# A joint network's forward and backward pass: rows of the second chunk by TensorE transposes, fe transposes planned later, grad x by two taps per matmul, last gradients reordered

## The chip, the core and the metric

The kernel runs on one core of a Trainium2 chip. A core has five engines that work side by side, each through its own queue in order: TensorE (matmuls into PSUM; PE in the profile, its weight loads PEld), VectorE (DVE), ScalarE (ACT), GpSimd (POOL) and SyncE (SP), which here only issues transfers. Transfers are carried out by 16 DMA engines that all queues share. The metric is the device time of one execution in microseconds (us).

## The reference

The kernel computes the forward pass below and the gradients of all seven inputs for a given `grad_out` (eight outputs in bfloat16). x is [2, 16000, 256], g is [2, 8, 256], and w1 and w2 have three taps of 256x256.

```python
h = gelu(conv3(x, w1))[:, ::2, :]          # tanh form of gelu; [2, 8000, 256]
f = gelu(conv3(h, w2))[:, ::2, :]          # [2, 4000, 256]
fe = einsum("btd,de->bte", f, w_f)
ge = einsum("bud,de->bue", g, w_g)
j = tanh(fe[:, :, None, :] + ge[:, None, :, :])   # [2, 4000, 8, 256]
out = einsum("btud,dv->btuv", j, w_o)
# and vjp of this: grads of x, w1, w2, g, w_f, w_g, w_o
```

## The kernel before

**Tiling.** The 2 x 4000 steps t of the output are cut into 17 chunks: the first of 256 steps, fifteen of 512, the last of 64. A chunk has A blocks (2, 4, 1) of at most 128 steps. Each chunk goes through three stages. Stage a (`stage_a`) computes the two convolutions with their gelu (`conv_gelu`): HTo and HTe (odd and even rows of h), FT (f), then FE (fe). All of these have features on partitions and steps along the free axis. Stage j (`stage_j`) forms j for the eight u, writes the output, and multiplies `grad_out` back to the gradient NGFE of fe. Stage de (`stage_de`) goes back through both convolutions: GF, GHe and GHo are the gradients before the gelus, `wgrad` adds the weight gradients up, and grad x is written row by row. The main loop over k puts stage j of chunk k beside stage a of chunk k+1 and stage de of chunk k-1.

**The order is planned.** Every operation is a call of `op` with an engine (or two that it may run on), a cost in ns, what it reads and writes, and a due time (`at`, else `F.now`). `Flow.issue` then simulates the engines with these costs, and at each step takes the operation that can start earliest, among equals the one due first; the order found is the program's order on each engine. An operation can start when what it depends on is done (`ready`). So a change of a cost, or of one operation, can move others in the queues far behind it. Transfers are `op`s too, on SP, ACT or POOL (`dma`).

**Two forms of j.** The output and the elementwise gradients need j with features on partitions: JT, by ACT's tanh of FE with ge as bias (L643). The gradient of w_o needs j with steps on partitions as well, the rows JR: two halves of the blocks for each of four pairs of u, so eight JR of 128x1024 in a full chunk. For chunks in `TRANS` they come from JT by TensorE transposes and one copy from PSUM (L662 and `evac`, L345 on ACT or L350 on DVE). For the other chunks TensorE transposes FE once (`rows`, L489), a copy makes FER, and then DVE adds ge's rows (L667) and ACT takes tanh again (L672). Before, `TRANS` is (0,). JR and grad_out's rows GO then go into the sum GWO in PSUM.

**What else the change touches.** `conv_gelu` takes Square (L510) and Gelu (L512) of each of two PSUM tiles, both due at `F.now`, Square first. Grad x (four rows per block) is made in pairs of rows: the first pair is GHo·tap0 + GHe·tap2 and GHo·tap1, the second pair is GHe'·tap0 + GHo·tap2 and GHe'·tap1 (GHe' is the block one further); each product has two halves of the contraction, so a pair takes six matmuls of 256 columns, into the two halves of one PSUM tile. In the chunk with the batch border, GHz, a copy of GHe with a zeroed column, stands for GHe' in tap 0 of block 0. Then the three taps of grad w1 follow. In the last chunk `acc_add` makes each weight gradient's final value by one DVE operation (L763) into a staging tile, and SP stores it.

Of the kernel before, what the change touches and what calls it, by code (L numbers as in the profile page):

```python
# [31 lines left out]
class Op:  # L32
    __slots__ = ("eng", "cost", "fn", "deps", "soft", "succ", "left", "prio", "new", "bufs", "done", "work", "n",
                 "ready", "kind", "span")


class Flow:
# [29 lines left out]

    def op(self, eng, cost, fn, r=(), w=(), new=(), at=None, work=0.0, after=(), kind=None, behind=(), sub=None):
        o = Op()
# [3 lines left out]
        o.prio = ((self.now if at is None else at) + self.shift.get((self.stage, sub), 0.0), o.n)  # L73
        o.succ, o.done, o.ready, o.kind, o.span = [], None, 0.0, kind, None
        deps, bufs = set(after), []
# [31 lines left out]
    def issue(self):  # L107
# [12 lines left out]
        def put(o):  # L120
            o.ready = max((d.span[0] if d in o.soft else d.done for d in o.deps), default=0.0)
            for e in o.eng:
                avail[e].append(o)
# [97 lines left out]
def kernel(  # L221
# [20 lines left out]
    B, T, D = x.shape  # L242
# [20 lines left out]
    SHIFT = {}  # L263
    TRANS = (0,)

# [214 lines left out]

    def rows(k, cls, name, SRC, lo, n, r, at=None, pe=0):
        R = buf(cls, [P, n if cls != "hro" else NB + 1, D], BF16, name)
        if pe:
            tr = psum(BF16)

            def trs(e):
                for a in range(n):
                    for kt in range(KT):
                        nc.tensor.transpose(out=tr[:pe, a * D + kt * P:a * D + (kt + 1) * P], in_=SRC[:, lo + a, kt, :pe],  # L489
                                            identity=ident[:])  # L490
            op("PE", c_pe([P] * (n * KT)), trs, r=(r or [SRC]) + [ident], w=[tr], new=[tr], at=at)
            evac(lambda: R[:pe, 0:n].rearrange("p a d -> p (a d)"), lambda: tr[:pe, 0:n * D], n * D, r=[tr], w=[R], new=[R], f=0.58)
            return R
        dma("SP", lambda: R[:, 0:n].rearrange("p a (k d) -> p (a k) d", d=P),
            lambda: SRC[:, lo:lo + n].rearrange("p a k c -> p (a k c)"), r=[SRC] if r is None else r, w=[R],
            bytes_=n * 65536, new=[R], transpose=True, at=at)
        return R

    def conv_gelu(c, taps, rd, h_buf, h_lo, g_buf, g_lo, news):
# [3 lines left out]
        for mt in range(KT):  # L503
            ps = psum()

            def mms(e, mt=mt, ps=ps):
# [3 lines left out]
            op("ACT", c_act(W, True), lambda e, mt=mt, ps=ps: nc.scalar.activation(  # L510
                out=sq[:, 0:A, mt, :Pw], in_=fl(ps[:, :W], A), func=ACT.Square, scale=GELU_SQRT_K), r=[ps], w=[(sq, mt)])
            op("ACT", c_act(W, True), lambda e, mt=mt, ps=ps: nc.scalar.activation(  # L512
# [24 lines left out]
    def stage_a(k, t0, dt):  # L537
# [53 lines left out]
        if k not in TRANS:  # L591
            S["FER"] = rows(k, "fer", "FER", FE, 0, A, [(FE, 0), (FE, 1)], pe=Pw)
        F.now = t0 + 0.5 * dt
# [163 lines left out]
    def acc_add(ACC, key, acc_ap, ps, k, out):  # L757
        if k == NG - 1:
            t_ = buf({id(ACCF): "jr", id(ACC2): "jt", id(ACC1): "go"}[id(ACC)], [P, 2 * D], BF16, "stage")

            def flat():
# [3 lines left out]
                op0=ALU.mult, op1=ALU.subtract), r=[(ACC, key), ps], w=[t_], new=[t_])  # L765
            dma("SP", lambda: out.rearrange("(dt p) n -> p dt n", p=P),
                lambda: flat().rearrange("p (k d) -> p k d", d=D), r=[t_], w=[], bytes_=131072)
# [7 lines left out]
    def stage_de(k, t0, dt):  # L775
# [112 lines left out]
        if c.px is not None:  # L888
# [5 lines left out]
                r=[GHz], w=[GHzR], bytes_=65536, transpose=True)  # L894
        rows4 = [[(GHo, 0, 0), (GHe, 0, 2)], [(GHo, 0, 1)], [(GHe, 1, 0), (GHo, 0, 2)], [(GHe, 1, 1)]]
        GX = None
        for bl, m in c.sblk:
            if bl % 2 == 0:
                GX = buf("gx", [P, 2, 4, D], BF16, "GX_SB")
            for cp in range(2):  # L900
                ps = psum()
                jobs = []
                for cj in range(2):
                    l = [(SRC, off, i, kt) for SRC, off, i in rows4[2 * cp + cj] for kt in range(KT)]
                    jobs += [(cj, n == 0, n == len(l) - 1) + a for n, a in enumerate(l)]

                def mms(e, jobs=jobs, ps=ps, bl=bl, m=m):
                    for cj, s_, e_, SRC, off, i, kt in jobs:
                        src = SRC[:, off + bl, kt, :m]
                        if GHz is not None and bl == 0 and off == 1 and i == 0:  # L910
                            src = GHz[:, kt, :m]
                        mm(ps[:m, cj * D:(cj + 1) * D], src, W1T[:, kt, i * D:(i + 1) * D], s_, e_)
                op("PE", c_pe([D] * len(jobs)), mms, r=[GHo, GHe, W1T] + ([GHz] if GHz is not None else []), w=[ps],
                   new=[ps] + ([GX] if cp == 0 and bl % 2 == 0 else []))
# [3 lines left out]
            if bl % 2 == 1 or bl == A - 1:  # L918
# [14 lines left out]
                if c.ext and h == 0:  # L933
                    put(Pw, Pw + 1, 0, 3)
        for i in range(KK):
            def xl(da):
                return lambda a, m, d2: X[:m, 4 * a + da, d2 * P:(d2 + 1) * P]

            def he(a, m, i=i):
                return GHzR[:m, :] if GHzR is not None and i == 0 and a == 0 else GHeR[:m, a, :]  # L940
            wgrad(ACC1, i, lambda i=i: ACC1[:, i],
                  [(xl(i), rr(GHoR), c.sblk, [X, GHoR]),
                   (xl(i + 2), he, c.sblk, [X, GHeR] + ([GHzR] if GHzR is not None else []))], out_2[i])
            tick()

# [182 lines left out]
```

## Time and profile before

| what | us |
|---|---|
| median of three runs (lowest, highest) | 798.06 (797.32, 798.76) |
| the profiled execution, its own time | 797.41 |
| its span in the profile | 795.6 |
| busy: TensorE, VectorE, ScalarE, GpSimd | 774.8, 725.2, 720.7, 67.5 |
| mean granted TensorE clock | 0.996 of full speed |
| read from and written to memory | 51.42 and 50.34 MB |

The span begins with the first instruction and ends with the last; the execution's own time has about 1.8 us more around it. A busy TensorE is not TensorE at its peak: the ends of matmuls are modelled and overlap (one of 512 columns stands with 0.379 us while the next starts 0.216 us after it). So work on TensorE is counted here by the pitch from start to start, taken from rows with many matmuls. A row of the profile names line, engine, operation, output and inputs, then shapes, times and, in brackets, idle time before it and what ended it.

### The profile page before, as it was taken

What the parts mean: (1) busy time and instruction counts of PE and PEld (TensorE: products, weight loads), DVE (VectorE), ACT (ScalarE), POOL (GpSimd) and SP (SyncE); (2) the same over time, 40 slices, a digit from 0 to 9 for tenths busy, and PEclk for the clock granted to TensorE, in tenths of its full rate; (3) what the DMA queues carried; (4) which work ended last, traced back from release to release, by engine and by line L of the source; (5) the groups of instructions that cost most, each with busy time, mean ns of one, the idle gap of its engine ahead of it and who ended that gap; (6) DMA issues with size and microseconds to landing.
All of it is one profiled execution on the core that took longest, in us unless ns stands there. A gap on an engine that the chain in (4) does not pass through costs nothing.

```text
span 795.6 us, 16104 instructions
## 1 busy us (share of the span) xinstructions
PE 774.8 (97%) x5916; PEld 559.2 (70%) x5916; DVE 725.2 (91%) x1535; ACT 720.7 (91%) x1164; POOL 67.5 (8%) x227
## 2 busy tenths in 40 slices
PE   7989899999999999999999999999999999999996
PEld 6657578676776767768576685767868677687875
DVE  5899999998989989899998998989989999999964
ACT  6999999999898998989989899898999989899742
POOL 2020100101000010210100001010010100102010
PEclk9999999999999999999999999999999999999999
DMA  9999999999999999999999999999999999899994
GB/s 195 213 193 206 249 233 230 259 220 221 218 248 234 231 220 205 238 248 214 230 250 239 202 225 219 242 251 229 216 235 254 235 212 212 211 261 202 261 205 123
DMA packets 381811, 178.85 MB, mean 225 GB/s; under 512 B 307586, under 2 KB 375460, under 8 KB 379812
## 3 DMA queue, kind: packets, MB, share of 16 engines
q1 hardware_dynamic: 380788, 177.16, 99.7%
q8 instruction: 46, 0.75, 0.4%
q10 hardware_dynamic: 784, 0.39, 0.2%
q14 instruction: 33, 0.27, 0.1%
q0 software_dynamic: 160, 0.27, 0.1%
HBM read 51.42 MB, written 50.34 MB: 128 GB/s over the span
## 4 chain that ended last, share of the span: by engine, by line
PE 55%; ACT 24%; DVE 14%; issue 4%; DMA 3%; SPq 0%; DVEq 0%; ACTq 0%
PE ps L336 45%; PE GWO L336 8%; ACT JT L643 5%; ACT JR L672 4%; ACT JSQ L702 4%; ACT OUT_SB L345 3%; DVE g_s L515 3%; DVE NGZ L715 2%; ACT GX_SB L347 2%; ACT g_sq L510 1%; DVE ZS L732 1%; DMA GO<-in_grad_out_dram 1%; PE psb L489 1%; DMA out_dram<-OUT_SB 1%; DVE ACC L771 1%
## 5 line engine op out<-in xcount | busy, mean ns | idle before, releaser
L643 ACT ACTIVATE JT<-FE,GE 128x512 bf16<-128x512 bf16 (+4 forms) x288 | 190.7, 723 | 0.3 <-PE ps L336 0.3
L715 DVE SCALAR_TENSOR_TENSOR NGZ<-JSQ,ps 128x512 f32<-128x512 bf16 (+3 forms) x252 | 152.3, 613 | 1.6 <-PE ps L336 1.5
L336 PE MATMUL ps<-WO,JT 128*128 128x256 bf16 (+1 forms) x1008 | 150.0, 274 | 0.7 <-ACT JT L643 0.6
L336 PE MATMUL ps<-GOT,WOT 128*128 128x512 bf16 (+2 forms) x544 | 149.3, 363 | 0.4 <-DMA GOT<-GO 0.4
L672 ACT ACTIVATE JR<-JR 128x1024 bf16<-128x1024 bf16 (+1 forms) x124 | 136.2, 1101 | 12.8 <-DVE JR L667 12.8
L345 ACT CAST OUT_SB<-ps 128x512 bf16<-128x512 f32 (+1 forms) x215 | 132.7, 629 | 12.7 <-PE ps L336 12.5
L336 PEld LDWEIGHTS <-JT 128*128 128x128 bf16 (+1 forms) x1008 | 98.8, 98 | 57.9 <-issue 1.3
L702 ACT ACTIVATE JSQ<-JT 128x1024 bf16<-128x1024 bf16 (+2 forms) x123 | 128.7, 1046 | 10.0 <-DVE NGZ L715 7.7
L336 PE MATMUL GWO<-GO,JR 128*128 128x256 bf16 (+1 forms) x1008 | 131.4, 274 | 4.5 <-ACT JR L672 4.3
L732 DVE TENSOR_TENSOR ZS<-ZS,NGZ 128x1024 f32<-128x1024 f32 (+2 forms) x102 | 115.8, 1135 | 0.5
L336 PEld LDWEIGHTS <-JR 128*128 128x128 bf16 (+1 forms) x1008 | 98.0, 98 | 24.1 <-ACT JR L672 6.3
L336 PEld LDWEIGHTS <-W 128*128 128x128 bf16 x612 | 57.9, 98 | 59.7 <-issue 2.8
L515 DVE SCALAR_TENSOR_TENSOR g_s<-g_sq,ps 128x512 bf16<-128x512 bf16 (+2 forms) x102 | 65.1, 641 | 34.0 <-ACT HTo L512 32.7
L667 DVE TENSOR_TENSOR JR<-FER,GEB 128x1024 bf16<-128x1024 bf16 (+1 forms) x124 | 84.1, 684 | 3.1 <-PE GWO L336 2.3
L336 PE MATMUL ps<-XC,W 128*128 128x512 bf16 (+2 forms) x408 | 84.5, 362 | 1.7 <-DMA XC<-in_x_dram 1.7
L336 PEld LDWEIGHTS <-X 128*128 128x128 bf16 (+1 forms) x756 | 73.9, 98 | 9.0 <-DMA HRo<-HTo 0.2
L771 DVE TENSOR_TENSOR ACC<-ACC,ps 128x512 f32<-128x512 f32 x90 | 60.8, 684 | 20.1 <-PE ps L336 19.3
L336 PE MATMUL ps<-W1T,GHo 128*128 128x256 bf16 (+1 forms) x378 | 72.1, 273 | 0.0
L336 PE MATMUL ps<-W1T,GHe 128*128 128x256 bf16 (+1 forms) x376 | 71.8, 273 | 0.0
L510 ACT ACTIVATE g_sq<-ps 128x512 bf16<-128x512 f32 (+2 forms) x102 | 62.2, 610 | 8.6 <-PE ps L336 6.0
L336 PEld LDWEIGHTS <-WOT 128*128 128x128 bf16 x544 | 51.8, 98 | 22.9 <-DMA GOT<-GO 0.7
L347 ACT ACTIVATE GX_SB<-ps 128x512 bf16<-128x512 f32 (+1 forms) x98 | 59.2, 640 | 5.4 <-PE ps L336 4.9
(139 smaller groups left out, 1123.4 us busy)
## 6 DMA issues: line engine op xcount, KB each, us to landing
GO<-in_grad_out_dram SPq DMA_DIRECT2D x60, 512.0 KB, 5.6
out_dram<-OUT_SB SPq DMA_DIRECT2D x60, 512.0 KB, 6.1
X<-in_x_dram SPq DMA_DIRECT2D x15, 1088.0 KB, 7.4
out_dram<-GX_SB SPq DMA_DIRECT2D x30, 512.0 KB, 4.5
GO<-in_grad_out_dram SPq DMA_DIRECT2D x5, 256.0 KB, 5.3
GOT<-GO SPq DMA_TRANSPOSE x65, 4.7
out_dram<-OUT_SB SPq DMA_DIRECT2D x4, 256.0 KB, 3.5
XC<-in_x_dram SPq DMA_TRANSPOSE x62, 4.4
```

Of the source, the lines that this page charges most:

```text
L336: nc.tensor.matmul(ps_ap, lhsT=lhsT, rhs=rhs, start=start, stop=stop)
L345: nc.scalar.copy(out=dst(), in_=src())
L347: nc.scalar.activation(out=dst(), in_=src(), func=ACT.Copy, scale=scale)
L510: op("ACT", c_act(W, True), lambda e, mt=mt, ps=ps: nc.scalar.activation(out=sq[:, 0:A, mt, :Pw], in_=fl(ps[:, :W], A), func=ACT.Square, s ...
L515: op("DVE", c_dve(W), lambda e, mt=mt, ps=ps: nc.vector.scalar_tensor_tensor(out=s[:, 0:A, mt, :Pw], in0=sq[:, 0:A, mt, :Pw], scalar=1.0, ...
L643: nc.scalar.activation(out=fl(JT[:, j, mt, :W], A)[:, :, lo:hi], in_=FE[:, 0:A, mt, lo:hi], func=ACT.Tanh, bias=GE[:, b, mt, 2 * up + j:2 ...
L667: op("DVE", c_dve(n * 2 * D, 0.5), lambda e, lo=lo, n=n, m=m, JR=JR: nc.vector.tensor_tensor(out=JR[:m, 0:n], in0=S["FER"][:m, lo:lo + n]. ...
L672: op("ACT", c_act(n * 2 * D), lambda e, n=n, m=m, JR=JR: nc.scalar.activation(out=JR[:m, 0:n], in_=JR[:m, 0:n], func=ACT.Tanh), r=[JR], w= ...
L702: nc.scalar.activation(out=JSQ[:, :, :W], in_=JT[:, j, :, :W], func=ACT.Square)
L715: nc.vector.scalar_tensor_tensor(out=fl(zap(), A)[:, :, lo:hi], in0=fl(JSQ[:, d2, :W], A)[:, :, lo:hi], scalar=1.0, in1=fl(ps[:, :W], A)[: ...
L732: nc.vector.tensor_tensor(out=a, in0=a, in1=b, op=ALU.add)
L771: op("DVE", c_dve(512), lambda e: nc.vector.tensor_tensor(out=acc_ap().rearrange("p k d -> p (k d)"), in0=acc_ap().rearrange("p k d -> p ( ...
```

## The change

- `TRANS` is (0, 1): chunk 1, the first full one, makes JR from JT by transposes, and makes no FER.
- `op` has a new argument `lag`, which is added to the time at which the planner takes the operation as ready. The fe transposes of all chunks that still have them get 500 ns.
- In chunk 0, Square is due 8 ns later than Gelu.
- Grad x: of each pair, one source feeds two taps that lie side by side in W1T, so a matmul of 512 columns makes both rows; the other source adds 256 columns to the first row. Four matmuls in place of six; for GHz the 512 are split again. Both rows share one start mark.
- In the last chunk taps 0 and 1 of grad w1 come before grad x, tap 2 after it; tap 2's store goes by ACT's queue.

```diff
-    TRANS = (0,)
+    TRANS = (0, 1)
...
-    def op(self, eng, cost, fn, r=(), w=(), new=(), at=None, work=0.0, after=(), kind=None, behind=(), sub=None):
+    def op(self, eng, cost, fn, r=(), w=(), new=(), at=None, work=0.0, after=(), kind=None, behind=(), sub=None, lag=0.0):
...
-            o.ready = max((d.span[0] if d in o.soft else d.done for d in o.deps), default=0.0)
+            o.ready = max((d.span[0] if d in o.soft else d.done for d in o.deps), default=0.0) + o.lag
...
-            op("PE", c_pe([P] * (n * KT)), trs, r=(r or [SRC]) + [ident], w=[tr], new=[tr], at=at)
+            op("PE", c_pe([P] * (n * KT)), trs, r=(r or [SRC]) + [ident], w=[tr], new=[tr], at=at, lag=lag)
...
             op("ACT", c_act(W, True), lambda e, mt=mt, ps=ps: nc.scalar.activation(
-                out=sq[:, 0:A, mt, :Pw], in_=fl(ps[:, :W], A), func=ACT.Square, scale=GELU_SQRT_K), r=[ps], w=[(sq, mt)])
+                out=sq[:, 0:A, mt, :Pw], in_=fl(ps[:, :W], A), func=ACT.Square, scale=GELU_SQRT_K), r=[ps], w=[(sq, mt)],
+               at=F.now + 8.0 if c.first else None)
...
-            S["FER"] = rows(k, "fer", "FER", FE, 0, A, [(FE, 0), (FE, 1)], pe=Pw)
+            S["FER"] = rows(k, "fer", "FER", FE, 0, A, [(FE, 0), (FE, 1)], pe=Pw, lag=0.0 if c.first else 500.0)
...
-            dma("SP", lambda: out.rearrange("(dt p) n -> p dt n", p=P),
+            dma("ACT" if ACC is ACC1 and key == KK - 1 else "SP", lambda: out.rearrange("(dt p) n -> p dt n", p=P),
...
-        rows4 = [[(GHo, 0, 0), (GHe, 0, 2)], [(GHo, 0, 1)], [(GHe, 1, 0), (GHo, 0, 2)], [(GHe, 1, 1)]]
+        pairs4 = [(GHo, 0, GHe, 0), (GHe, 1, GHo, 0)]
+        def grad_w1(i):
...
+        for i in range(2 if c.last else 0):
+            grad_w1(i)
...
-                    for cj, s_, e_, SRC, off, i, kt in jobs:
-                        src = SRC[:, off + bl, kt, :m]
-                        if GHz is not None and bl == 0 and off == 1 and i == 0:
-                            src = GHz[:, kt, :m]
-                        mm(ps[:m, cj * D:(cj + 1) * D], src, W1T[:, kt, i * D:(i + 1) * D], s_, e_)
-                op("PE", c_pe([D] * len(jobs)), mms, r=[GHo, GHe, W1T] + ([GHz] if GHz is not None else []), w=[ps],
+                    z = GHz is not None and bl == 0 and cp == 1
+                    for kt in range(KT):
+                        if z:
+                            mm(ps[:m, 0:D], GHz[:, kt, :m], W1T[:, kt, 0:D], kt == 0, False)
+                            mm(ps[:m, D:2 * D], SA[:, oa + bl, kt, :m], W1T[:, kt, D:2 * D], False, False)
+                        else:
+                            mm(ps[:m, 0:2 * D], SA[:, oa + bl, kt, :m], W1T[:, kt, 0:2 * D], kt == 0, False)
+                    for kt in range(KT):
+                        mm(ps[:m, 0:D], SB[:, ob + bl, kt, :m], W1T[:, kt, 2 * D:3 * D], False, kt == KT - 1)
+                op("PE", c_pe([2 * D] * 2 + [D] * 2), mms, r=[GHo, GHe, W1T] + ([GHz] if GHz is not None else []), w=[ps],
...
-        for i in range(KK):
+        for i in range(2 if c.last else 0, KK):
+            grad_w1(i)
```

## The prediction

> **What bounds the kernel now.** I read the page first, then the busy time by stretches, then the waits, then rows in order of time where a wait was long.
>
> The page: shares of the span, and what they say when set against the stretches (start:end, length, then busy time of PE, PEld, DVE, ACT, POOL, granted clock, DMA share, GB/s).
>
> ```profile
> PE 774.8 (97%) x5916; PEld 559.2 (70%) x5916; DVE 725.2 (91%) x1535; ACT 720.7 (91%) x1164; POOL 67.5 (8%) x227
> ...
> 140.00:188.00 48.00, 47.95 (x361) 34.50 (x359) 45.04 (x89) 45.13 (x70) 3.69 (x12) 1.00 1.01 227
> ...
> 334.00:760.00 426.00, 424.20 (x3236) 307.17 (x3235) 398.80 (x827) 393.64 (x637) 31.64 (x114) 1.00 1.01 232
> ```
>
> From about 92 us to 760 us TensorE is the bound: it is busy 424.2 of 426 us. Time saved there is work taken off TensorE or a wait taken away from it; work taken from DVE or ACT is worth nothing there.
>
> Chunk 1's joint stage, about 40 to 92 us, is different. Its waits (weight loads and what they waited for, with total, times, longest) and its rows, both from 38 to 92 us:
>
> ```profile
> PEld L336 <- ACT JR L672: 6.3, 5, 2.2
> ...
> L672 ACT ACTIVATE JR<-JR 128x1024 bf16<-128x1024 bf16 x10 | 10.9, 1109 | 0.3 <-DVE JR L667 0.3
> L667 DVE TENSOR_TENSOR JR<-FER,GEB 128x1024 bf16<-128x1024 bf16 x10 | 6.9, 693 | 0.0
> ```
>
> The stretches show ACT busy 50.8 and DVE 50.4 of these 52 us, so here the two of them are the bound and TensorE waits, mostly for the row tanh (JR). One pause is long enough to halve TensorE's clock:
>
> ```profile
> 42.00:44.00 2.00, 0.70 (x5) 0.29 (x3) 2.00 (x7) 2.00 (x5) 0.00 (x0) 1.00 1.07 153
> 44.00:45.00 1.00, 0.12 (x1) 0.11 (x2) 1.00 (x4) 1.00 (x2) 0.00 (x0) 1.00 1.27 207
> 45.00:46.00 1.00, 1.00 (x7) 0.74 (x6) 1.00 (x3) 1.00 (x2) 0.15 (x1) 0.55 1.26 207
> 46.00:47.00 1.00, 1.00 (x6) 0.72 (x5) 1.00 (x6) 0.87 (x2) 1.00 (x4) 0.50 1.28 238
> 47.00:48.00 1.00, 1.00 (x5) 0.46 (x3) 1.00 (x5) 0.51 (x2) 0.54 (x1) 0.50 1.28 216
> 48.00:49.00 1.00, 1.00 (x8) 0.73 (x7) 0.38 (x2) 1.00 (x3) 0.00 (x0) 0.74 0.64 118
> ```
>
> Four slices miss 0.45+0.50+0.50+0.26 = 1.7 us of full clock. With the 6.3 us of waits, about 8.0 us of TensorE time are lost in this stage.
>
> In the steady part (100 to 760 us) one wait stands out, that of the fe transposes for FE's eviction; below it one such place in order of time:
>
> ```profile
> PEld L489 <- ACT FE L345: 5.2, 11, 0.9
> ...
> 258.89 0.61 PE L489 MATMUL psb<-ident,FT 128*128 128x128 bf16 x8
> 259.64 1.05 ACT L345 CAST FE<-ps 128x512 bf16<-128x512 f32 x2
> 260.26 0.23 PE L489 MATMUL psb<-ident,FE 128*128 128x128 bf16 x1 [0.76 <-ACT FE L345]
> 260.75 0.56 PE L489 MATMUL psb<-ident,FE 128*128 128x128 bf16 x7 [0.26 <-ACT FE L345]
> 261.15 0.38 PE L336 MATMUL ps<-W1T,GHo 128*128 128x256 bf16 x2
> ```
>
> The work that stands behind the transposes (grad x, W1T) was ready and had to queue. And the end, where engine time turns into stores:
>
> ```profile
> 788.79 1.88 DVE L763 SCALAR_TENSOR_TENSOR stage<-ACC,ps 128x512 bf16<-128x512 f32 x3 [0.20 <-PE ps L336]
> 789.50 0.96 SPq L362 DMA_DIRECT2D out_dram<-GX_SB  x2
> 790.56 1.73 SPq L362 DMA_DIRECT2D out_dram<-stage  x3
> ```
>
> The span ends at 795.6; after the last issue (792.3) comes only its landing and the closing.
>
> **The change part by part.** The profiled execution took 797.41 us (span 795.6 and 1.8 around it), 0.65 under the median 798.06; the sum is made on 797.41 and 0.65 put back at the end.
>
> *Rows of chunk 1 by transposes.* Removed: 8 DVE adds of 0.693 (5.5 us), 8 ACT tanh of 1.109 (8.9), one FER copy on DVE (0.7), 8 fe transposes. Added: 64 transposes, and 8 copies of 128x1024 from PSUM. Chunk 0 already has both: eight transposes stand as 0.61 us, of which one is 0.22, so the pitch is (0.61-0.22)/7 = 0.056; the copy takes 0.696 on DVE and 1.037 on ACT. TensorE gains 56 x 0.056 = 3.1 us of work. ACT and DVE together lose 15.1 and get 8 copies, some 7.0 if half go to each: 8.1 us less over two engines, 4.0 off a stretch that both fill. TensorE would allow 52 - 8.0 + 3.1 = 47, about the same. Three engines that each need 47 to 48 never interlock perfectly, so I take -3.0. Ends: -4.9 (all 8.0 of waits gone against 3.1 of work) and +3.1 (no wait recovered). The new wait: transposes wait for all four JT of the pair, and behind them on TensorE queue the WO, WOT and GWO matmuls; the copies wait for TensorE, and behind them on ACT or DVE everything else. After 92 us TensorE is full, so what is won is kept.
>
> The trace has eight transposes in 0.61 us, chunk 0's among them. The Trainium skill, "TensorE: Matmul & The Clock Gate", section "Part 4: PE-mode transpose", gives about 275 ns for one in a kernel, and says that transposes do not count as activity for the clock in the way that matmuls do. By the first figure this term would be an estimated 15.4 in place of 3.1 and the sum 802; the trace does not agree, and the row is used.
>
> *fe transposes later.* The planner treats them as ready 0.5 us later than it thinks FE done; the work behind them goes first. The 11 waits of 5.2 us lie in eight chunks, up to two in one (0.76 and 0.26 above, by the PE row). Half a microsecond covers most of each, at most 8 x 0.5 = 4.0; I take -3.5. Ends: -5.2, and +0.5 if a pause comes up elsewhere. What hides the delay: the first JR add that needs FER starts 6.5 to 10.5 us after FER's copy ended from chunk 3 on (e.g. 262.0+1.03 to 272.75), but only 1.6 us in chunk 2 (84.43+0.70 to 86.77). Should that cover go, DVE stalls 0.5 once.
>
> *Two taps per matmul.* Per row block and pair: six matmuls of 256 columns before, two of 512 and two of 256 after. Pitches: sixteen of 256 in 1.91 us, (1.91-0.27)/15 = 0.109; 24 of 512 in 5.34, (5.34-0.38)/23 = 0.216. 0.655 against 0.650, 5 ns x 126 = -0.6. Weight loads (98 ns) are hidden either way, so 250 fewer (the one group with GHz keeps six) are worth nothing. Ends 0 and -0.8.
>
> *Square after Gelu in chunk 0.* The second Gelu of HTe and that of FT (rows 10.55 and 12.88) stand one Square (0.27 from start to start) behind; both are in the chain to the first fe matmul at 13.32: up to -0.54. The sigma branch on DVE gets its Square 0.27 later. From 14 us ACT works without a pause, so an earlier start is worth something: -0.3, ends -0.54 and +0.3.
>
> *The end.* Taps 0 and 1 of grad w1 come before the last grad x, so the three DVE adds (1.88 in a row from 788.79) no longer follow the last matmul; only one does: TensorE still ends at 789.6, the last add at 790.3 and not 790.7. Its store leaves by ACT's queue, where nothing but the closing drain is behind it. SP has then four issues of some 0.45 after its last data, not five, the fifth of which waited 0.4 for a free semaphore. Grad x and its two ACT evictions come 0.87 later (eight matmuls of 0.109) and their two stores become SP's last, ending near 791.3 and not 792.3: -1.0. Ends -1.4 and +0.4.
>
> Sum: -3.0 - 3.5 - 0.6 - 0.3 - 1.0 = -8.4; 797.4 - 8.4 = 789.0, on the median **789.7**.
>
> **Rivals.** *Chunk 1 gains nothing:* copies land on ACT (1.037 for 1.109) and the planner's pauses only change their name. For it: ACT is the fuller engine there. Against: DVE is 5.5 us lighter and can take them. 789.7 + 3.0 = 792.7.
>
> *The delay does not do what it says:* other work was already planned between FE and its transposes, or the chip drifts from the plan by as much at another place. For it: by the rows above FE was late by 1.0 us in all, more than the 0.5. 789.7 + 3.5 = 793.2.
>
> *Slower: TensorE stalls at the transposed rows.* Each half's chain is now ACT, TensorE, ACT or DVE, TensorE, in queues that run in order. If each of the 8 halves stalls TensorE for x, chunk 1 costs 8x + 3.1 against the 8.0 lost now; the other parts bring 5.4. It is slower from 8x = 10.3, x = 1.3 us each. Today's five waits have a mean of 1.26 and reach 2.2; at 1.8 the time is 798.1 + 14.4 + 3.1 - 8.0 - 5.4 = 802.2. Against it: chunk 0 does the same with waits of 0.2 in all.
>
> *The clock:* transposes as pauses. Each pause like the one at 42 to 45 costs 1.7 us of clock; one per half is 8 x 1.7 = 13.6, so 803.3, from five on it is slower. In chunk 0's transposes, 17 to 36 us, the clock stays at 1.00. The Trainium skill's rule on activity, in the page and section named above, is this rival; the trace does not bear it out.
>
> **How the numbers follow.** Forecast 0.60 (its own range 786 to 792), chunk 1 nothing 0.14, delay without effect 0.11, stalls 0.12, clock 0.03. A measurement here tells 0.2%, 1.6 us, from no change. The first three are faster, less a little for two of them together: faster 0.83, same 0.04, slower 0.13. Range: all best ends together are -12.8, 785.2, so 785.5 below; upwards past both failures together (796.2) to 797, which leaves the stalls and the clock out.
>
> **What would show it.** Chunk 1: no L672 and L667 before chunk 2, 96 transposes of JT, no 0.50 clock near 45, about 3 us less until the 92 us point. The delay: fe transposes after W1T or other matmuls, the wait for FE under 1.7 us. Two taps: W1T matmuls 128x512, TensorE's count 5916 - 250 + 56 = 5722. The end: grad w1's last add alone after the last matmul, an ACT store, some 1 us less from last matmul to end. I am wrong if waits for a copy from psb or for a PSUM bank replace those for JR, or if the steady part has new waits from the newly dealt order.

## The result, and the profile after

The changed kernel takes 794.21 us (median of 20 executions, 792.0 to 797.84), the kernel before 798.67 us beside it (20 executions, 797.08 to 800.8). The ratio is 0.9947, with a 95% interval of 0.9935 to 0.9959: faster by 4.2 us. The forecast was 8.4 us. The direction was right and the time lies in the range, but the gain is half of what was forecast, and the experiments below find next to nothing of this half in the terms that were summed.

The profiled execution after took 793.30 us, with a span of 791.0. The page's first part, and the stretches that answer to those shown of before (length, busy time of PE, PEld, DVE, ACT, POOL, granted clock, DMA share, GB/s):

```profile
PE 773.1 (98%) x5687; PEld 537.9 (68%) x5722; DVE 716.1 (91%) x1514; ACT 727.0 (92%) x1176; POOL 83.8 (11%) x227
...
42.00:44.00 2.00, 1.06 (x13) 0.82 (x14) 2.00 (x7) 2.00 (x4) 0.00 (x0) 1.00 1.04 182
44.00:45.00 1.00, 0.07 (x1) 0.07 (x1) 1.00 (x4) 1.00 (x3) 0.00 (x0) 1.00 1.25 251
45.00:46.00 1.00, 1.00 (x10) 0.89 (x10) 1.00 (x4) 1.00 (x3) 0.79 (x2) 1.00 1.28 227
...
334.00:760.00 426.00, 423.72 (x3083) 294.22 (x3104) 392.30 (x812) 401.14 (x652) 44.17 (x118) 1.00 1.01 231
```

The weight loads are 5722, the count that was forecast (35 matmul records are missing from this trace). The steady part is full as before. The clock near 45 us is 1.00 and not 0.50; more on that below. The pause at 42 to 45 us is still there: TensorE is busy 1.13 of these 3 us, while VectorE and ScalarE are busy all the time.

Chunk 1's joint stage: the rows of its eight copies from 38 to 92 us, and then the places where TensorE pauses, in order of time. The last line is of before: what its matmuls there waited for JR.

```profile
L345 ACT COPY JR<-psb 128x1024 bf16<-128x1024 bf16 x6 | 6.2, 1053 | 0.0
...
L350 DVE COPY JR<-psb 128x1024 bf16<-128x1024 bf16 x2 | 1.4, 681 | 0.0
```

```profile
42.08 0.45 PE L663 MATMUL psb<-ident,JT 128*128 128x128 bf16 x5 [0.90 <-ACT JT L644]
43.05 0.61 PE L663 MATMUL psb<-ident,JT 128*128 128x128 bf16 x8 [0.52 <-DVE NGZ L716]
44.93 1.03 PE L336 MATMUL ps<-WO,JT 128*128 128x256 bf16 x8 [1.27 <-DVE NGZ L716]
...
89.26 1.04 PE L336 MATMUL ps<-GOT,WOT 128*128 128x512 bf16 x4 [1.57 <-DMA GOT<-GO]
...
PE GWO L336 <- ACT JR L672: 4.3, 3, 1.7
```

The waits for JR are gone: 6.3 us in the weight loads' rows, 4.3 in those of the matmuls. In their place TensorE's matmuls wait for JT, for VectorE's NGZ and for the transfer GOT, and for as long: 0.90 + 0.52 + 1.27 + 1.57 = 4.3 us. Six of the eight copies went to ScalarE, which was the fuller engine.

In the steady part the waits for FE, 5.2 us before, are gone. The largest wait of the weight loads from 100 to 740 us is now:

```profile
PEld L336 <- issue: 3.0, 9, 0.5
```

The place shown of before at 259 us looks so in order of time after, with FE's two halves taken by ScalarE and VectorE side by side and eight matmuls of other work (0.9 us by their pitch) ahead of the transposes:

```profile
256.56 0.57 ACT L345 CAST FE<-ps 128x512 bf16<-128x512 f32 x1
...
256.70 0.68 DVE L350 CAST FE<-ps 128x512 bf16<-128x512 f32 x1
...
257.18 1.04 PE L336 MATMUL ps<-NFR,FR 128*128 128x256 bf16 x8
...
258.05 0.61 PE L489 MATMUL psb<-ident,FE 128*128 128x128 bf16 x8
```

And the end, in order of time:

```profile
784.78 1.88 DVE L764 SCALAR_TENSOR_TENSOR stage<-ACC,ps 128x512 bf16<-128x512 f32 x3 [0.45 <-PE ps L336]
...
785.34 0.27 PE L336 MATMUL ps<-GHeR,X 65*128 65x256 bf16 x1
...
786.61 1.14 SPq L362 DMA_DIRECT2D out_dram<-stage  x2
786.70 0.42 ACTq L362 DMA_DIRECT2D out_dram<-stage  x1
```

Three adds still stand in a row, as before, and are not done when the last matmul is. Grad x was not moved behind two taps. The one thing that is new is the store on ACT's queue.

**Where the 4.6 us between the two spans lie.** TensorE's time is split at 38, 100 and 740 us into work by pitch (0.216, 0.109 and 0.056 us for 512, 256 and 128 columns; the 35 matmuls without a record are counted in) and what is lost between pitches. The lost time of a slow clock, one minus the granted clock per microsecond, is shown apart. The same sums were made for the experiments.

| us | 0-38 lost | 38-100 lost | of it slow clock | 100-740 lost | 740 to last matmul lost | after last matmul | span |
|---|---|---|---|---|---|---|---|
| before | 6.8 | 8.7 | 1.7 | 7.4 | 3.3 | 6.3 | 795.6 |
| after | 6.2 | 5.7 | 0 | 3.7 | 4.4 | 5.7 | 791.0 |
| rows_only | 6.7 | 6.5 | 1.7 | 5.9 | 3.6 | 6.2 | 795.2 |
| delay_only | 7.0 | 7.4 | 0 | 8.5 | 3.5 | 6.2 | 795.6 |
| taps_same_order | 6.9 | 9.1 | 1.7 | 7.7 | 3.8 | 6.2 | 796.3 |
| taps_new_order | 6.8 | 7.5 | 0 | 5.6 | 4.0 | 5.8 | 792.2 |
| all_but_rows | 6.2 | 9.9 | 1.7 | 4.0 | 4.0 | 5.7 | 792.1 |
| end_enforced | 6.8 | 5.6 | 1.7 | 3.8 | 5.6 | 4.3 | 791.7 |

After against before: in 38 to 100 us 3.0 less is lost, 1.7 of it slow clock, but the transposes add 56 x 0.056 = 3.1 us of work, so nothing is won there. From 100 to 740 us 3.7 less is lost, and the taps' pitches save 0.6. The opening and the time after the last matmul bring 0.6 each, and the stretch before the last matmul gives 1.1 back. So the gain lies in the steady part, and the question for the experiments is which edit put it there.

The times of the two profiled executions differ by 4.1 us and not 4.6, since 2.3 us lie outside the span after and 1.8 before; why is not shown. And each row is one execution: cost_told_only below runs the order of taps_new_order and loses 1.5 us less from 100 to 740 us by the same sum, so a difference of that size between two rows is not yet one between two kernels.

### The profile page after: what moved, and what is told of

Its sections match the earlier page's. It is cut to its first block, busy times and chain, and to the rows that moved or that the text cites. A ratio compares the mean times of both kernels' runs of the same rounds, so it can differ in the third digit from the quotient of the medians.

```text
span 791.0 us, 15682 instructions
## 1 busy us (share of the span) xinstructions
PE 773.1 (98%) x5687; PEld 537.9 (68%) x5722; DVE 716.1 (91%) x1514; ACT 727.0 (92%) x1176; POOL 83.8 (11%) x227
## 4 chain that ended last, share of the span: by engine, by line
PE 72%; ACT 11%; DVE 9%; DMA 3%; issue 3%; SPq 1%; POOL 0%; DVEq 0%; ACTq 0%
PE ps L336 60%; PE GWO L336 10%; ACT JT L644 2%; DVE g_s L516 2%; ACT JSQ L703 2%; DMA GOT<-GO 2%; ACT g_sq L510 2%; PE psb L489 2%; DVE NGZ L716 1%; ACT OUT_SB L345 1%; ACT JR L673 1%; DVE g_sq L529 1%; SPq L360 1%; ACT HTo L513 1%; DMA XC<-in_x_dram 1%
## 5 line engine op out<-in xcount | busy, mean ns | idle before, releaser
L644 ACT ACTIVATE JT<-FE,GE 128x512 bf16<-128x512 bf16 (+4 forms) x288 | 180.7, 680 | 0.0
L716 DVE SCALAR_TENSOR_TENSOR NGZ<-JSQ,ps 128x512 f32<-128x512 bf16 (+3 forms) x252 | 149.7, 607 | 2.5 <-PE ps L336 2.0
L336 PE MATMUL ps<-WO,JT 128*128 128x256 bf16 (+1 forms) x1008 | 148.2, 273 | 1.3 <-DVE NGZ L716 1.3
L336 PE MATMUL ps<-GOT,WOT 128*128 128x512 bf16 (+2 forms) x544 | 146.5, 362 | 1.8 <-DMA GOT<-GO 1.6
L345 ACT CAST OUT_SB<-ps 128x512 bf16<-128x512 f32 (+1 forms) x210 | 123.0, 600 | 17.4 <-PE ps L336 17.3
L336 PEld LDWEIGHTS <-JT 128*128 128x128 bf16 (+1 forms) x1008 | 98.2, 98 | 54.9 <-issue 2.0
L336 PE MATMUL GWO<-GO,JR 128*128 128x256 bf16 (+1 forms) x1008 | 130.8, 273 | 0.1
L673 ACT ACTIVATE JR<-JR 128x1024 bf16<-128x1024 bf16 (+1 forms) x116 | 121.6, 1054 | 4.1 <-DVE JR L668 3.8
L336 PEld LDWEIGHTS <-JR 128*128 128x128 bf16 (+1 forms) x1008 | 98.2, 98 | 17.8 <-issue 1.3
L336 PEld LDWEIGHTS <-W 128*128 128x128 bf16 x612 | 58.1, 98 | 59.5 <-issue 2.2
L336 PE MATMUL ps<-XC,W 128*128 128x512 bf16 (+2 forms) x408 | 84.3, 362 | 0.9 <-DMA XC<-in_x_dram 0.9
L668 DVE TENSOR_TENSOR JR<-FER,GEB 128x1024 bf16<-128x1024 bf16 (+1 forms) x116 | 79.2, 684 | 2.2 <-PE GWO L336 1.0
L336 PEld LDWEIGHTS <-X 128*128 128x128 bf16 (+1 forms) x756 | 73.8, 98 | 9.4
L336 PEld LDWEIGHTS <-WOT 128*128 128x128 bf16 x544 | 51.6, 98 | 23.9 <-DMA GOT<-GO 1.8
L347 ACT ACTIVATE GX_SB<-ps 128x512 bf16<-128x512 f32 (+1 forms) x109 | 64.1, 615 | 1.6 <-PE ps L336 1.1
L510 ACT ACTIVATE g_sq<-ps 128x512 bf16<-128x512 f32 (+2 forms) x102 | 59.1, 580 | 3.4 <-PE ps L336 2.7
L525 ACT ACTIVATE g_s<-g_s 128x1024 bf16<-128x1024 bf16 (+2 forms) x51 | 52.1, 1025 | 6.3 <-DVE g_s L516 6.1
L336 PE MATMUL ps<-GHoR,X 128*128 128x256 bf16 (+1 forms) x378 | 57.7, 273 | 0.0
```

What stands on the lines that cost most here:

```text
L336: nc.tensor.matmul(ps_ap, lhsT=lhsT, rhs=rhs, start=start, stop=stop)
L345: nc.scalar.copy(out=dst(), in_=src())
L347: nc.scalar.activation(out=dst(), in_=src(), func=ACT.Copy, scale=scale)
L644: nc.scalar.activation(out=fl(JT[:, j, mt, :W], A)[:, :, lo:hi], in_=FE[:, 0:A, mt, lo:hi], func=ACT.Tanh, bias=GE[:, b, mt, 2 * up + j:2 ...
L668: op("DVE", c_dve(n * 2 * D, 0.5), lambda e, lo=lo, n=n, m=m, JR=JR: nc.vector.tensor_tensor(out=JR[:m, 0:n], in0=S["FER"][:m, lo:lo + n]. ...
L673: op("ACT", c_act(n * 2 * D), lambda e, n=n, m=m, JR=JR: nc.scalar.activation(out=JR[:m, 0:n], in_=JR[:m, 0:n], func=ACT.Tanh), r=[JR], w= ...
```

## The experiments: one part alone, or all but one

Ratios are to the kernel before, run beside each, with 95% intervals.

**Rows alone.** Of the whole change only

```diff
-    TRANS = (0,)
+    TRANS = (0, 1)
```

> The kernel before with TRANS = (0, 1) alone. Theory L (loads gate chunk 1: between 41 and 47 us TensorE has nothing else loaded, so the waits for JR become waits for JT, PSUM and GOT): stretch up to 92 us as long as before, waits down by about as much as the 3.1 us of transposes, total within 1 us of before. Forecast's own view (ACT and DVE bound the stretch): 3.0 us faster.

Measured: 0.9981 (0.9972 to 0.9990), -1.5 us. Its pauses at chunk 1's entry, in order of time:

```profile
42.62 0.45 PE L662 MATMUL psb<-ident,JT 128*128 128x128 bf16 x5 [0.90 <-ACT JT L643]
43.59 0.61 PE L662 MATMUL psb<-ident,JT 128*128 128x128 bf16 x8 [0.52 <-DVE NGZ L715]
45.47 0.95 PE L336 MATMUL ps<-WO,JT 128*128 128x256 bf16 x4 [1.27 <-DVE NGZ L715]
```

The waits that take the place of JR's are those of the changed kernel, to the hundredth. The stretch to 100 us loses 2.2 us less than before and has 3.1 us more to do. What the kernel gained as a whole lies behind it, where it lost 5.9 in place of 7.4 us: the order of later chunks was dealt anew as well, and its wait there for FE fell from 5.2 to 0.6 us although no fe transpose was delayed.

**All but the rows.** The changed kernel with `TRANS = (0,)`.

> The changed kernel with TRANS = (0,) again. Theory L: like the changed kernel, 4.2 us faster than before, within 1 us. Forecast's own view: 3.0 us slower than the changed kernel, so about 1 us faster than before.

Measured: 0.9949 (0.9935 to 0.9962), -4.1 us. Without the rows the change is worth as much as with them.

**The delay alone.** Only `lag=500.0` for the fe transposes from chunk 1 on.

> The kernel before with the 500 ns delay of the fe transposes alone. If the delay is what brought the gain: 3.5 us faster, no waits of TensorE for FE's eviction in the steady part. If the newly dealt order alone did it (rival R): the waits for FE stay or others take their place, and the time is within 1.5 us of before.

Measured: 1.0017 (1.0003 to 1.0031), +1.4 us. Its waits from 100 to 740 us, and then the place at 259 us in order of time:

```profile
PEld L489 <- ACT FE L345: 4.7, 12, 0.5
PEld L336 <- issue: 3.3, 8, 0.9
```

```profile
259.23 0.38 PE L336 MATMUL ps<-W1T,GHo 128*128 128x256 bf16 x2
...
260.19 0.56 PE L489 MATMUL psb<-ident,FE 128*128 128x128 bf16 x7 [0.26 <-ACT FE L345]
```

The delay does its work at this place: grad x goes ahead and the pauses of 0.76 and 0.26 become 0.26. But over the steady part twelve shorter waits for FE replace eleven, and the waits at L336 under "issue" rise from 0.7 to 3.3 us; 8.5 us are lost in place of 7.4. The profiled execution was the fastest of twelve (797.42 us; the median is 800.19), so it does not show the whole of the 1.4.

**All but the delay.** The changed kernel with `lag=0.0`.

> The changed kernel with a delay of zero. If the delay brought the gain: about 0.7 us faster than before, with 3 to 5 us of waits for FE's eviction back. Rival R: still about 4 us faster.

Measured: 0.9947 (0.9933 to 0.9961), -4.2 us, the same as with it. Its wait for FE is 0.9 us. So the delay is not what took these waits away. But this kernel is hardly another one: from 100 to 740 us, 99% of the instructions of VectorE and of ScalarE stand in the same order with the delay as without. In the changed kernel the delay moves next to nothing, and what it is worth by itself is seen in delay_only.

**Two taps, with the order of before.** Grad x in four matmuls, but the planner is still told the cost of six, 655 ns and not 650. The instructions of VectorE, ScalarE, GpSimd and SyncE then stand exactly in the order of before. Against the changed kernel's line:

```diff
-                op("PE", c_pe([2 * D] * 2 + [D] * 2), mms, ...
+                op("PE", c_pe([D] * 6), mms, ...
```

> The kernel before with two taps per matmul alone, and the planner told the old cost, so that every engine keeps its old order. Theory P (the taps are worth their pitch): 0.6 us faster, too little to measure. Theory W (fewer weight loads or matmuls are worth more than their pitch, and the taps are what made the changed kernel faster): 3 to 4 us faster with the same waits for FE as before.

Measured: 1.0003 (0.9989 to 1.0017): nothing. It has 250 fewer matmuls and weight loads than before, and the wait for FE is 5.4 us.

**Two taps, with the cost as changed.** The same matmuls; the planner is told 650 ns.

> The same with the planner told the new cost (5 ns less per group), so that it deals a new order. Theory P with theory R (what a part seems to bring is mostly the newly dealt order): differs from the kernel with the old order by 1 us or more, with other waits for FE. Theory W: the same 3 to 4 us.

Measured: 0.9948 (0.9931 to 0.9965), -4.1 us. The two kernels differ in 5 ns of a planned cost and in the order that follows from it. This one edit brings as much as the whole change. Its order is not that of the changed kernel, though: of the instructions of VectorE and ScalarE from 100 to 740 us, 63 to 66% stand in the same order in both (86 to 89% in this kernel and before). And of the 3.4 us that its row of the table is shorter than that of before, 1.7 are the slow clock that its execution did not have. Its wait for FE from 100 to 740 us:

```profile
PEld L489 <- ACT FE L345: 2.2, 6, 0.7
```

**Square after Gelu alone.**

> The kernel before with Square due after Gelu in chunk 0 alone. By the forecast's term: first fe matmul at 12.8 instead of 13.32, 0.3 us faster. Theory R: the opening gains that, but the order dealt after it moves the total by up to 2 us to either side.

Measured: 1.0001 (0.9988 to 1.0014): nothing. The first fe matmul starts at 14.16 us and not at 12.8, but in this profiled execution TensorE runs at half speed until 10.1 us (matmuls of 256 columns follow at 0.213 us, and at 0.109 after that), so the term cannot be read here. From 100 to 740 us the order changes in one or two of a hundred instructions.

## The experiments: what in the new order brings the gain

**The cost alone, with before's matmuls.** The kernel before, with one number changed:

```diff
-                op("PE", c_pe([D] * len(jobs)), mms, ...
+                op("PE", c_pe([2 * D] * 2 + [D] * 2), mms, ...
```

> The kernel before with its six matmuls, the planner told 650 ns for them in place of 655: ACT, DVE, POOL and SP run exactly the order of the kernel with two taps and newly dealt order, TensorE the same order of groups. Theory D (the dealt order alone brought the 4.1 us): 3.0 to 4.5 us faster than before. Rival (taps and order are needed together, since six matmuls take the 5 ns longer that the planner was not told): under 1.5 us faster.

Measured: 0.9954 (0.9938 to 0.9971), -3.7 us. It computes grad x just as before, with six matmuls, in the order of taps_new_order on the four other engines. So the order is what is faster, and the two-tap matmuls are not needed for it. Its wait for FE:

```profile
PEld L489 <- ACT FE L345: 2.1, 6, 0.7
```

**Other told costs.** taps_new_order with 645 and with 660 ns told (the edit for 645):

```diff
-                op("PE", c_pe([2 * D] * 2 + [D] * 2), mms, ...
+                op("PE", c_pe([D] * 6) - 10.0, mms, ...
```

> Two taps, the planner told 645 ns per group: another deal, real instructions unchanged. If any deal with less time told on TensorE does it: 4 us faster than before. If deals scatter: anywhere from 1 us slower to 5 us faster.

> Two taps, the planner told 660 ns per group: another deal. If telling more time does harm: no faster than before. If deals scatter: from 1 us slower to 5 us faster.

Measured: 0.9975 (0.9961 to 0.9988), -2.0 us, for 645; 1.0022 (1.0012 to 1.0033), +1.8 us, for 660 (`+ 5.0` in place of `- 10.0`). With 655, 0.0, and 650, -4.1, the same matmuls give four times, with no trend by the number told. The wait of the fe transposes for ScalarE's FE goes with it in part: 7.1 us at 660 and 5.4 at 655, 2.6 and 2.2 at 645 and 650.

**Is it ScalarE's queue in front of FE?** In before, a row tanh of 1.1 us (L672) often stands directly ahead of an FE eviction on ScalarE. The next kernels hold such a tanh back until the evictions behind it are out; all other engines keep their order (the lines that set the tags are left out here).

```diff
...
-            o.fn(e)
+            if hold is not None and (hold in o.deps or (e == "ACT" and o.tag != "FE")):
+                hold.fn("ACT")
+                hold = None
+            if e == "ACT" and o.tag == "JRT":
+                hold = o
+            else:
+                o.fn(e)
...
```

> The kernel before with one thing changed: where ACT's queue has a JR tanh directly ahead of FE's evictions, the evictions go first; every other engine keeps its order to the instruction. Theory Q (TensorE waits for FE because FE's eviction stands on ACT behind a JR tanh that waits for a late DVE add): the wait for FE's eviction in the steady part falls from 5.2 to under 1 us, and the time by 3.5 to 5 us, without any part of the change. Rival: ACT as a whole is late, the wait falls by less than half and the time by less than 1.5 us, or GWO's wait for JR takes its place.

Measured in the kernel before: 1.0000 (0.9984 to 1.0015). The steady part's waits (the edit moves line numbers by nine; L498 is the fe transpose, L345 the matmul, L354 and L359 the evictions), and below them two of the same rows before:

```profile
PEld L345 <- issue: 3.6, 7, 1.0
PEld L498 <- DVE FE L359: 2.4, 4, 1.2
PEld L498 <- ACT FE L354: 1.0, 2, 0.7
...
PEld L336 <- issue: 0.7, 3, 0.4
PEld L489 <- DVE FE L350: 0.3, 2, 0.2
```

The wait for FE by ScalarE falls from 5.2 to 1.0 us, as was aimed at, and the time does not move: VectorE's FE and "issue" (a wait that the profile puts down to nothing) take its place: 2.1 and 2.9 us more for 4.2 less. The largest wait in the steady part of this kernel was a symptom and not a price.

> The same swap in the kernel with two taps and the newly dealt order (4.1 us faster than before, waits for FE 2.2 + 0.5). Theory Q: waits for FE under 0.7 and another 1.5 to 2.5 us, so about 6 us faster than before. Rival: no change beyond 1 us.

Measured in taps_new_order: 0.9952 (0.9936 to 0.9968), -3.8 us, no more than without the swap.

> The same swap in the changed kernel with TRANS = (0,). If rows by transposes are worth nothing of their own (3.1 us of TensorE work against some 3 us of waits) and only dealt an order without JR ahead of FE: some 2 us faster than the changed kernel's 4.2, so about 6. If rows are worth 3 us: slower than the changed kernel or equal to it.

Measured in all_but_rows: 0.9949 (0.9931 to 0.9966), -4.1 us, again as without it.

## The experiments: the rows' stage and the end

**The copies on VectorE.** The changed kernel, with all of chunk 1's eight copies on VectorE, where one takes 0.68 us and not 1.05:

```diff
-                         lambda tr=tr, n=n, m=m: tr[:m, 0:n * 2 * D], n * 2 * D, r=[tr], w=[JR], new=[JR], f=0.58)
+                         lambda tr=tr, n=n, m=m: tr[:m, 0:n * 2 * D], n * 2 * D, r=[tr], w=[JR], new=[JR], f=0.58,
+                         eng=("ACT", "DVE") if k == 0 else "DVE")
```

> The changed kernel with chunk 1's eight row copies on DVE alone (six of eight were on ACT). If chunk 1 gained nothing because ACT stayed full with the copies: TensorE's pauses between 38 and 100 us fall by 2 us or more and the time with them. Theory L (loads and JT gate): pauses at 41 to 45 us and for GOT near 89 stay, 5 to 6 us in all, and the time is within 1 us of the changed kernel's.

Measured: 0.9930 (0.9912 to 0.9949), -5.6 us, the fastest complete kernel here, though its interval overlaps that of the changed kernel. Its order from 100 to 740 us is the changed kernel's but for one instruction of VectorE and one of ScalarE. The wait for GOT near 89 us is gone; those of 0.90, 0.52 and 1.27 us at 41 to 45 us are not.

**Chunk 1 entered without rows.** The changed kernel with the first pair's transposes, copies and GWO matmuls left out, to see whether the rows make this pause (the line that corrects the count of GWO matmuls is left out here).

```diff
...
-            for h, tbs in enumerate(halves):
+            for h, tbs in enumerate(halves if not (k == 1 and up == 0) else []):
```

> The changed kernel with the rows of chunk 1's first pair left out: its 16 transposes, two copies and 16 GWO matmuls (so the gradient of w_o lacks them). If the pause of TensorE at 41 to 45 us belongs to the rows: it goes from 3.2 us to under 1. If it belongs to the entry into chunk 1 (JT late on ACT, PSUM held by chunk 0's NGZ on DVE, nothing else loaded): 2.5 us or more of pauses stay between 40 and 48 us.

Measured, in two executions: 0.9864 (0.9846 to 0.9881), -10.9 us, of which the work left out explains 16 x 0.056 + 16 x 0.109 = 2.6. The pauses at chunk 1's entry stay, as its order of time on TensorE shows:

```profile
43.92 0.28 PE L336 MATMUL ps<-WO,JT 128*128 128x256 bf16 x1 [0.75 <-ACT JT L644]
44.90 0.60 PE L336 MATMUL ps<-WO,JT 128*128 128x256 bf16 x4 [0.69 <-DVE NGZ L716]
46.56 0.59 PE L336 MATMUL ps<-GOT,WOT 128*128 128x512 bf16 x2 [1.06 <-ACT OUT_SB L345]
```

0.75 + 0.69 + 1.06 = 2.5 us, against 0.90 + 0.52 + 1.27 = 2.7 with the rows. So this pause does not belong to the rows. ScalarE and VectorE are full there; that they are its cause was not tried by itself. The rest of the gain lies in the steady part again, where this kernel loses only 1.1 us: another deal.

**The end made to be what was described.** The changed kernel, with grad x of the last chunk placed in the program behind taps 0 and 1 (the line that names these taps' operation is left out here):

```diff
...
-                   new=[ps] + ([GX] if cp == 0 and bl % 2 == 0 else []))
+                   new=[ps] + ([GX] if cp == 0 and bl % 2 == 0 else []),
+                   behind=[S["wop"]] if c.last else [])
```

> The changed kernel with grad x of the last chunk really planned behind taps 0 and 1 of grad w1 (the changed kernel itself runs grad x first). If the forecast's working of the end was right once the order is real: one DVE add after the last matmul and not three, last issue 0.5 to 1 us earlier against the last matmul than in the changed kernel, 4.7 to 5.2 us faster than before. Rival: grad x's evictions and stores become the last, and the end is as long as in the changed kernel, 4.2 us faster than before.

Measured: 0.9945 (0.9928 to 0.9963), -4.4 us, as the changed kernel. In order of time:

```profile
784.85 0.27 PE L336 MATMUL ps<-GHoR,X 65*128 65x256 bf16 x1 [1.03 <-ACT GHoR L345]
...
787.66 0.69 DVE L764 SCALAR_TENSOR_TENSOR stage<-ACC,ps 128x512 bf16<-128x512 f32 x1 [0.89 <-PE ps L336]
...
788.38 0.39 ACTq L362 DMA_DIRECT2D out_dram<-stage  x1
```

Now one add alone follows the last matmul, and the time after that matmul falls by 1.35 us, from 5.66 to 4.31. But the taps need GHoR, which ScalarE has yet to copy, and with grad x no longer ahead of them TensorE stands still for 1.03 us. Grad x had been the cover of this copy.

## Why the prediction was wrong

The sum priced each wait as time that comes back when its cause is taken away, with the rest of the order held fixed. That step failed: 6.5 of the forecast 8.4 us stood on the rows and on the delay, and both times other waits took the place of those removed. What moves the time by microseconds in the runs that tell a new cost alone is the order that the planner deals, and the sum had no term for it. So it is luck that the sign was right and the time lies in the range: another deal of the same kind (660 ns told) was 1.8 us slower.

**Rows of chunk 1, forecast -3.0, shown near 0.** The working at the instructions holds: eight transposes stand as 0.61 us, the copies took 1.05 and 0.68 us, the counts are right. The step that failed is "TensorE would allow 52 - 8.0 + 3.1 = 47", which took all 8.0 us of lost time as recoverable and asked only whether VectorE and ScalarE could follow. Without slow clock, the five whole kernels with the new rows lose 3.4 to 5.7 us in this stretch (mean 4.7), the twelve with the old rows 7.0 to 8.2 (mean 7.6). So 2.9 come back, and the transposes take 3.1. The entry's 2.5 us are there with or without rows (entry_without_rows), and the other 1.7, the slow clock, hangs on the execution and not on the kernel alone (last section). "Half each" for the copies failed too: six of eight went to ScalarE, and putting them on VectorE took the late GOT wait away. The rival "Chunk 1 gains nothing" named this, with the copies on ScalarE and "pauses only change their name".

**fe transposes later, forecast -3.5, shown 0 or worse.** The 5.2 us of waits did go, but the delay alone gives +1.4 us, and in the changed kernel it moves next to nothing and costs nothing to take out. The step that failed is "Half a microsecond covers most of each": it priced each wait as if the rest of the order would stay. At the one place shown it was right; the same planner then put its shortages elsewhere. swap_in_before shows it without any new deal: with the wait removed by a swap on ScalarE alone, other waits of the same size appear. The rival "The delay does not do what it says" names this in its second form, "the chip drifts from the plan by as much at another place".

**Two taps, forecast -0.6, shown within 0.2% of 0 by itself.** Pitches and counts were as worked out, and -0.6 us is below what taps_same_order can tell. That 250 fewer weight loads are worth nothing was right. What the sum did not have is what the 5 ns do to the order: -4.1 us in taps_new_order and -3.7 in cost_told_only. The prediction reckoned with "new waits from the newly dealt order" only as a way to be wrong, with no term, no sign and no price. That is the missing term, and by itself it is the size of the whole result.

**Square after Gelu, forecast -0.3.** From the first XC matmul to the first fe matmul it is 12.54 - 6.39 = 6.15 us and not 6.75 as before. That is -0.6, near the better end, and it is so in all five profiled executions with the edit in which TensorE is at full speed from the first XC matmul on. What the stretch to 38 us keeps of it differs: the changed kernel and all_but_rows lose 6.2 us there where before loses 6.8, but end_enforced loses 6.8 too, and square_only gains nothing in the total. So the worth of it is not secured.

**The end, forecast -1.0, shown about -0.2.** The step that failed is "the three DVE adds (1.88 in a row from 788.79) no longer follow the last matmul": the change only writes the taps first in the text, and the planner, which takes what can start earliest, still put grad x first, since GHeR and GHoR were not there yet. What is left is the moved store. The time after the last matmul is 5.7 us in the changed kernel, but already 5.8 in taps_new_order, which has no edit at the end. The 1.1 us more that are lost ahead of the last matmul is there in taps_new_order for the most part too (4.0 against 3.3 us), so it came with the deal. Where the order is enforced, the forecast of the tail comes true (-1.35) and is paid back as a wait of 1.03; the sum had no such wait, and had not named what covers the copy of GHoR.

**Stalls and clock.** The two slower rivals did not come: the transposed rows add no stall for each half, and the clock is no worse than before; the rival's 1.7 us for each pause are paid only where the pauses fall so that one step has little work (last section). The rows speak against the 275 ns of the Trainium skill, "TensorE: Matmul & The Clock Gate", section "Part 4: PE-mode transpose", in chunk 1 as in chunk 0: eight of them stand as 0.61 us. Its rule that transposes do not count as activity in the way that matmuls do is not borne out here either (last section).

**What stays open.** That the order of the two-tap deal is faster by 4 us, and not the matmuls, is shown. Why one deal loses 3.7 us in the steady part and another 9.9 (660 ns told) is not: FE's waits go along with it, but removing them directly changed nothing. That the changed kernel's own 4.2 us come from its order is argued and not shown: its gain lies in the steady part, where the delay moves next to nothing and the taps' pitches are worth 0.6 us, but the changed kernel with 655 ns told was not run. It was also not tried what the parts are worth together under one fixed order.

## What to carry to other kernels

Where a planner writes the order, every edit of a cost or due time deals a new order, and that alone moved this kernel by +1.8 to -4.1 us: run the old code with only the new number, and the new code in the old order, before a gain is put down to an edit. Remove the largest wait by the smallest swap and see whether the time follows, since a wait on a full engine may only be where its shortage shows. A pause is put down to a piece of work only when a run without that work no longer has it, and a reordering counts only once it is seen in the instruction order, with a name for what covered the wait that it uncovers.

## What was not expected of the hardware

**The same pause halves the clock in one execution and not in another.** In the changed kernel and in rows_only TensorE has the same three pauses, 0.90, 0.52 and 1.27 us, ahead of 45 us (both shown above). The changed kernel's execution keeps a clock of 1.00; that of rows_only falls to half. These stretches show it, two of rows_only and then two of the changed kernel (the same columns as above):

```profile
42.15:45.56 3.41, 1.15 (x14) 0.92 (x15) 3.41 (x11) 3.41 (x6) 0.00 (x0) 1.00 0.94 168
45.56:48.97 3.41, 3.41 (x17) 2.42 (x17) 2.31 (x7) 3.14 (x6) 1.77 (x4) 0.50 1.13 220
...
39.73:43.14 3.41, 1.99 (x17) 1.10 (x15) 3.41 (x12) 3.41 (x6) 0.00 (x0) 1.00 1.03 192
43.14:46.55 3.41, 2.13 (x23) 1.85 (x23) 3.41 (x10) 3.41 (x6) 1.34 (x3) 1.00 1.22 213
```

The stretches are cut so for a reason. In all 18 profiled executions the granted clock changes in steps of 3.41 us (between the opening and the last matmuls each spell at half clock lasts 3.41 us, and each spell at full clock a whole number of them: 40.96 us are 12, 78.51 are 23). Where the steps begin differs from execution to execution. The work by pitch in a step goes with the clock of the next one: of the steps at full clock up to 780 us, the 13 that were followed by half clock have 1.30 us of work or less, and all others, over 4000, have 1.34 or more. In rows_only the pauses fall into one step, with 0.83 us of work; in the changed kernel they fall into two, with 1.5 and 2.0.

These sums count the transposes as work like any other. Without them they no longer part the steps: the changed kernel's at 39.73 us has 0.97 us of other matmuls and 0.53 of transposes and kept its clock, while steps with 1.19 and 1.23 us and no transposes lost it. So here the transposes count as activity.

Of the 18 executions eleven have such a stretch at half clock between 38 and 100 us, one of them two; each costs 1.7 us of full clock (the thirteenth lies at 7 us, in all_but_delay). It stands with the old rows (eight of twelve) and the new (three of six), near 46 or near 89 us. So the 1.7 us that the forecast hoped to regain at 45 us were one execution's, and the changed kernel's 20 executions have a mean granted clock of 0.9965, those of the kernel before 0.9963 over the 91 that ran beside the experiments.

**A few nanoseconds of a planned cost are worth microseconds.** Told costs of 645, 650, 655 and 660 ns for one matmul group gave -2.0, -4.1, 0.0 and +1.8 us with the same matmuls, while taking 250 weight loads away in the order of before gave 1.0003 (0.9989 to 1.0017).
